# Cosine attention with a token/channel mixer on one core: no dummy products in the first slots, one transpose moved to TensorE, SyncE's transposes ahead of its loads

## The chip, the cores and the metric

The kernel runs on one core of a Trainium2 chip. The metric is the device time of one execution in microseconds; less is better. A core has TensorE (PE, matrix products and transposes, with weight loads on a second track, PEld), VectorE (DVE), ScalarE (ACT), GpSimd (POOL) and SyncE (SP, here a queue that only issues transfers). ScalarE and GpSimd issue a few transfers too. Each engine works through its own instructions in order and waits on semaphores for the others.

## The reference, cut to what matters

```python
# q, k, v: (8, 12, 448, 64) float32;  tau = 0.1
q_n = q / (norm(q, axis=-1) + 1e-6);  k_n = k / (norm(k, axis=-1) + 1e-6)
attn = softmax(q_n @ k_n.T / tau)             # per batch and head, 448 x 448
x = (attn @ v), heads side by side            # (8, 448, 768)
u = x + (relu(x.T @ w_tok1) @ w_tok2).T       # mix over the 448 tokens, 256 hidden
out = u + relu(u @ w_ch1) @ w_ch2             # mix over the 768 channels, 1536 hidden
```

## The kernel before, in words

**Tiling.** The 12 heads of a batch are taken two at a time: a pair fills 128 channels. There are 6 pairs in a batch (`NPAIR`) and 48 in all (`NP_ALL`). The pairs 0 to 11 ("old") hold a head's 448 rows as 4 groups of 112 rows; from pair 12 on, K and V are held as 3 groups of 128 rows plus a rest of 64 (`KC` = 3, the tiles `kr` and `vr`, loaded once for three pairs).

**Stages of a pair.** `load_qk` and `load_v` bring q, k and v (SP's queue; k of pairs 0 to 2 on ACT's). `square` (L240 on POOL, L238 on ACT) squares q and k, `sums` (L263, DVE) adds the squares up, `norms` (L276 to L280 on ACT, L273 and L274 on DVE) makes 1/(norm + eps), `scale` (L292 to L300, POOL) multiplies q and k by it into `kq`, in float16. `tpose` transposes `kq` on TensorE (L316) and DVE copies the result out of PSUM into `qk` (L318); from pair 13 on (`DMA_T0`) `tpose_dma` does this with one transposing transfer on SP (L324). `score` makes the products of k and q (L339, and L346 for the rest of k), ACT takes the exponential into `pt` (L340, L347). `cast_v` (L216 to L220, POOL) makes v float16. `pv_wide`, or `pv_rest` and `pv`, multiply by v (L361, L378, L396); DVE divides by the sum (reciprocal L381 or L399, product L382 or L400) and gives `x`. `tok1` (L409, relu on DVE L412) and `tok2` (L423, added to x on DVE, L426) give `u`.

**The channel mix** needs u transposed, `ut`: `udma` does this with a transposing transfer on SP (L432), `upose` with four TensorE transposes and a DVE copy (L438, L439). `m_ch1` multiplies `ut` of a whole batch, all six pairs, by w_ch1 (L448, relu on ACT L451); `m_ch2` multiplies by w_ch2 (L464), adds u on DVE (L468) and stores (L483, L489).

**Order of work.** All instructions of an engine stand in the order in which the program calls these functions. The program is a loop over slots, one for each pair i, written out by hand:

- The slots 1 to 5 (L582 to L614) hold attention alone, since no batch is complete. On TensorE a slot is: two score groups, `tok1(i-2)`, `pv_wide(i-1)`, two score groups, `tpose(i+1)`, `tok2(i-2)`, and `warm(8)` (L608): eight 128-wide products of the identity matrix with itself, which nothing reads. On SP a slot ends with `load_v(i+4)` and `udma(i-2)` (L614).
- Slot 6 is written out at L616 to L635. Slot 7 starts with three score groups, `tok2(5)`, `upose(4)` and `upose(5)`, `sums(9)`, `pv(6, ...)`, and then the first unit of the channel mix of batch 0 (L666 to L684).
- From slot 7 on, a queue of units (12 `m_ch1` and 6 or 8 `m_ch2` for a batch) is fed into the slots by a budget of estimated TensorE time (`fed`, `due`, `refill`). So TensorE always has channel work of the batch before between the steps of attention.
- `side(i)` (L639 to L664) holds the work of the other engines in slot i: loads of pair i+6 or i+7, squares, `cast_v(i)`, norms, `scaled(i+2)`, `tpose_dma(i+2)` from slot 11 on, `load_v(i+4)`. On SP the order in a slot is therefore: loads of q and k, transpose of `kq` (which waits for POOL's `scaled`), load of v, then stores and the `udma` of that slot. On POOL it is: squares, cast, scaling. `SQ_AT` says which pairs are squared where the shift from i+3 to i+5 is made: slot 12 squares the pairs 15 and 16, slot 14 the pairs 18 and 19.

**Buffers.** q and k have 7 each, v has 4, `kq` has 4, `ut` 2. In PSUM the tag "b" has 2 buffers (transposes, tok1, tok2, pv, the dummy products, some channel units) and the tag "s" has 3 (scores and wide units).

**Weights** come through POOL's queue: w_ch1 in four parts (L193), w_ch2 in two (L197), cast on the way.

Of the kernel before, what the change touches and what calls it, by code (L numbers as in the profile page):

```python
# [8 lines left out]
FP16 = mybir.dt.float16  # L9
# [13 lines left out]
def kernel(  # L23
# [12 lines left out]
    nc = tc.nc  # L36
# [11 lines left out]
    NPAIR = H // 2  # L48
    NP_ALL = B * NPAIR
# [4 lines left out]
    DMA_T0 = 13  # L54
# [34 lines left out]
    ps = ctx.enter_context(tc.tile_pool(name="ps", bufs=2, space=bass.MemoryType.PSUM))  # L89
# [4 lines left out]
    ut = {}  # L94
    u16 = {}
    gts = {}

    def old(i):
        return i < OLD
# [22 lines left out]
    def load_qk(i):  # L122
        b, h0 = i // NPAIR, 2 * (i % NPAIR)
        n = i // HP
        half.setdefault(n, {})
        st = pipe[i] = {}
        st["q"] = qkv.tile([SC, QS, E], FP32, name=f"qf_{i}", tag="qf")
        nc.sync.dma_start(out=st["q"][:].rearrange("p (g c) e -> p g (c e)", g=2),
                          in_=q[b, h0:h0 + 2].rearrange("g (p c) e -> p g (c e)", c=NCH))
        st["k"] = load_rows(i, "k", k[b], 7)  # L130
        if not old(i) and "kr" not in half[n]:
            half[n]["kr"] = load_rest(i, "k", k[b])

    def load_v(i):
        pipe[i]["v"] = load_rows(i, "v", v[i // NPAIR], 4)
        if not old(i) and "vr" not in half[i // HP]:
            half[i // HP]["vr"] = load_rest(i, "v", v[i // NPAIR])

    id16 = cst.tile([128, 128], FP16, name="id16")
# [102 lines left out]
    def squares(i):  # L242
        square(i, 0)
        square(i, 1)
# [75 lines left out]
    def tpose_dma(i):  # L320
        st = pipe[i]
        qk = att.tile([128, 2 * NCH * 128], FP16, name=f"qk_{i}", tag="qk")
        st["qk"] = qk[:].rearrange("p (a c s) -> p a c s", a=2, c=NCH)
        nc.sync.dma_start_transpose(out=st["qk"].rearrange("p a c s -> p (a c) s"),  # L324
                                    in_=st["kq16"][:].rearrange("p a c g e -> p (a c g e)"))

    def warm(n, wide=False):
        w = (ps2 if wide else ps).tile([128, 128], FP32, name=f"warm{len(pipe)}_{n}", tag="s" if wide else "b")
        for _ in range(n):
            nc.tensor.matmul(w[:], id16[:], id16[:], start=True, stop=True)  # L330
# [100 lines left out]
        b, pj = i // NPAIR, i % NPAIR  # L431
        nc.sync.dma_start_transpose(out=ut[b][:, pj], in_=u16[b][:, pj].rearrange("p m d -> p (m d)"))  # L432

    def upose(i):
        b, pj = i // NPAIR, i % NPAIR
        psT = ps.tile([128, 4, 128], FP16, name=f"psT_{i}", tag="b")
        for m in range(4):
            nc.tensor.transpose(psT[:, m], u16[b][:, pj, m], id16[:])  # L438
        nc.vector.tensor_copy(out=ut[b][:, pj], in_=psT[:])  # L439

    def m_ch1(b, ct, wide):
        if b // 2 not in gts:
# [80 lines left out]
    SQ_AT = {12: [15, 16], 13: [17], 14: [18, 19], 15: [20]}  # L523
    SU_AT = {15: [18, 19]}

    with tc.manual_schedule():
        for i in range(3):
            load_qk(i)
        load_v(0)
        load_qk(3)  # L530
        load_v(1)
        load_qk(4)
        load_v(2)
        load_qk(5)
        load_v(3)
        nc.scalar.add_instruction(mybir.InstLoadActFuncSet(
            name=nc.get_next_instruction_name(), act_func_set_id=ACT_SET_LN_EXP,
            ins=[], outs=[]))
        weights_tok1()

        square(0, 1, act=True)
        square(0, 0, act=True)
        sums(0, 1, 2)
        norms(0, 1, 1, 2)
        sums(0, 0, 1)
        norms(0, 1, 1, 2, dve=True)
        norms(0, 1, 0, 1)
        scale(0, 1, nc.vector)
        norms(0, 1, 0, 1, dve=True)
        scale(0, 0)  # L550
        square(1, 1, act=True)
        square(1, 0, act=True)
        square(2, 1, act=True)
        warm(40, True)
        sums(1)
        norms(1, 2)
        tpose(0, 1, 2)
        warm(3, True)
        tpose(0, 0, 1)
        warm(5, True)  # L560
        square(2, 0)
        weights_tok2()
        score(0, 0)
        score(0, 1)
        norms(1, 2, dve=True)
        scale(1, 0)
        scale(1, 1, nc.vector)
        sums(2)
        norms(2, 3)
        cast_v(0)  # L570
        score(0, 2)
        warm(8)
        tpose(1)
        score(0, 3)
        warm(6)
        norms(2, 3, dve=True)
        square(3, 1, act=True)
        square(3, 0)
        load_v(4)
        load_qk(6)  # L580

        for i in range(1, NPAIR):  # L582
            if i == 1:
                scale(2, 0)
                scale(2, 1, nc.vector)
            else:
                scaled(i + 1)
                if i != 3:
                    weights_ch1(max(i - 3, 0))
            load_qk(i + 6)  # L590
            score(i, 0)
            score(i, 1)
            sums(i + 2)
            norms(i + 2, i + 3)
            if i >= 2:
                tok1(i - 2)
            pv_wide(i - 1)
            norms(i + 2, i + 3, dve=True)
            cast_v(i)
            square(i + 3, 0)  # L600
            if i == 1:
                warm(10)
            score(i, 2)
            score(i, 3)
            tpose(i + 1)
            if i >= 2:
                tok2(i - 2, pe=True)
            warm(8)  # L608
            square(i + 3, 1, act=True)
            if i == 1:  # L610
                place_w2()
            load_v(i + 4)
            if i >= 2:
                udma(i - 2)  # L614

        i = NPAIR  # L616
        load_qk(i + 6)
        scaled(i + 1)
        score(i, 0)
        score(i, 1)  # L620
        sums(i + 2)
        norms(i + 2, i + 3)
        tok1(i - 2)
        pv_wide(i - 1)
        norms(i + 2, i + 3, dve=True)
        cast_v(i)
        load_v(i + 4)
        squares(i + 3)
        scaled(i + 2)
        weights_ch1(3)  # L630
        score(i, 2)
        score(i, 3)
        tpose(i + 1)
        tok1(i - 1)
        tok2(i - 2, pe=True)  # L635

        def side(i):  # L639
            single = i + 2 < SINGLE  # L640
            t = i + (6 if i <= 14 else 7)
            if t < NP_ALL:
                load_qk(t)
            for t in SQ_AT.get(i, [i + 3 if single else i + 5]):
                if t < NP_ALL:
                    squares(t)
            cast_v(i)
            if i in (8, 10):
                weights_ch2((i - 8) // 2)
            if single:  # L650
                norms(i + 2, i + 3)
                norms(i + 2, i + 3, dve=True)
            elif i + 4 < NP_ALL:
                sums(i + 4)
                if (i + 4) % HP == 2:
                    norms(i + 2, i + 5, act=True)
            if i + 2 < NP_ALL:
                scaled(i + 2)
                if i + 2 >= DMA_T0:
                    tpose_dma(i + 2)  # L660
            if i + 4 < NP_ALL:
                load_v(i + 4)
            if i == 14:
                load_qk(i + 7)  # L664

        for i in range(NPAIR + 1, NP_ALL):  # L666
            b, pj = i // NPAIR, i % NPAIR
            for c in range(KC):
                score(i, c)
            if i == NPAIR + 1:  # L670
                tok2(i - 2, pe=True)
                upose(i - 3)
                upose(i - 2)
                sums(i + 2)
            pv_rest(i - 1)
            pv(i - 1, 0)
            pv(i - 1, 1)
            if i == NPAIR + 1:
                refill(0)
            elif pj == 2 and b > 1:  # L680
                refill(b - 1)
            side(i)
            fed[0] += fed[1]
            unit(True)  # L684
            if old(i):
                score(i, KC)
            else:
                score_rest(i)
            if i > NPAIR + 1:
                tok2(i - 2)  # L690
            if i + 1 < DMA_T0:
                tpose(i + 1)
            if due():
                unit(True)
            while due():
                unit()
            tok1(i - 1)
            if i + 2 < SINGLE:
                for t in SU_AT.get(i, [i + 3]):
                    sums(t)  # L700
        last = NP_ALL - 1
        unit()
        pv_rest(last)
        pv(last, 0)
        pv(last, 1)
        unit(True)
        tok2(last - 1)
        unit(True)
        tok1(last)
        unit(True)  # L710
        unit(True)
        tok2(last)
        refill(B - 1)
        while queue:
            unit()
# [35 lines left out]
```

## Time and profile before

| what | value |
|---|---|
| median of 7 runs | 399.38 us (393.63 to 403.48) |
| the profiled execution, own time | 393.67 us |
| its span, first to last instruction | 391.9 us |
| busy in the span: TensorE, weight loads, DVE, ACT, POOL | 375.0, 244.5, 209.1, 224.9, 237.1 us |
| moved by transfers | 65.13 MB, mean 166 GB/s |
| transposing transfers: `ut<-u`, `qk<-kq` | 46, 35 |
| dummy products (`warm`) | 112, of which 40 in the slots 1 to 5 |

1.8 us of the profiled execution's time lie outside its span. That execution is among the quickest: the seven runs reach from 0.04 us below it to 9.8 us above it.

How to read what follows: times in a timeline are microseconds from the start of the span; a row gives start, duration, engine, line, operation, output<-input, shape, how many instructions were merged, and in square brackets how long the engine stood idle before them and what ended that. In the page's rows of groups, busy time and the mean duration of one instruction (ns) stand after the first bar, the idle time ahead of the group and its main cause after the second. Matmuls are pipelined, so a mean duration is longer than the time from one start to the next.

### The profile page before, as it was taken

Reading aid. Unit: us, or ns where it says so; the run is one execution under the profiler, and the core shown is the slowest. Engines: PE = TensorE matmul, PEld = TensorE weight load, DVE = VectorE, ACT = ScalarE, POOL = GpSimd, SP = SyncE. Lnnn points to the kernel's source line nnn. Section 1 sums busy time; section 2 is a strip of 40 time slices with the busy share of each in tenths; the row PEclk is TensorE's granted clock in tenths of the full one; section 3 lists DMA queues with packets and bytes.
Section 4 is the critical chain, followed back from the end, with each engine's and each line's share of the span. In section 5 each row is a group of like instructions: output and inputs, shape, how many; then the busy total and the mean of one; then the engine's idle time right before and its main releaser. Section 6 shows DMA issues by size and latency. Waiting matters only on the chain.

```text
span 391.9 us, 10212 instructions
## 1 busy us (share of the span) xinstructions
PE 375.0 (96%) x4136; PEld 244.5 (62%) x4136; DVE 209.1 (53%) x457; ACT 224.9 (57%) x378; POOL 237.1 (60%) x384
## 2 busy tenths in 40 slices
PE   6989799998999999999999999999999999999995
PEld 5667566665656666666666666667666666565563
DVE  7788766676544575465544574465544553232032
ACT  5899678845574547764674547764674546601400
POOL 8899887897788492949677492949575440000000
PEclk9999999999999999999999999999999999999999
DMA  8999999988699989875899688786796382013023
GB/s 223 263 227 227 226 268 181 224 182 190 159 222 172 198 202 217 144 185 159 182 205 175 155 211 213 149 161 139 196 213 133 66 185 69 15 48 101 0 67 96
DMA packets 117599, 65.13 MB, mean 166 GB/s; under 512 B 75440, under 2 KB 113968, under 8 KB 117552
## 3 DMA queue, kind: packets, MB, share of 16 engines
q1 hardware_dynamic: 112656, 58.54, 68.5%
q0 software_dynamic: 4080, 5.21, 7.7%
q10 hardware_dynamic: 816, 0.73, 0.7%
q8 instruction: 32, 0.52, 0.6%
q14 instruction: 15, 0.12, 0.1%
HBM read 43.45 MB, written 11.01 MB: 139 GB/s over the span
## 4 chain that ended last, share of the span: by engine, by line
PE 81%; DMA 6%; DVE 6%; ACT 3%; issue 1%; POOL 1%; SPq 1%; ACTq 0%; DVEq 0%; POOLq 0%
PE psG L448 27%; PE psF L464 25%; PE psO L378 9%; PE psS L339 7%; PE psR L409 5%; PE psU L423 4%; DMA ut<-u 3%; DMA qf<-in_q_dram 2%; PE psQ L346 2%; ACT pt L340 2%; DVE ssq L263 1%; PE psO L361 1%; DMA kf<-in_k_dram 1%; DVE ost L468 1%; PE psO L396 1%
## 5 line engine op out<-in xcount | busy, mean ns | idle before, releaser
L340 ACT ACTIVATE pt<-psS 128x896 f16<-128x896 f32 (+1 forms) x156 | 132.6, 916 | 54.2 <-PE psS L339 54.1
L448 PE MATMUL psG<-ut,wc1t 128*128 128x448 f16 x576 | 116.9, 352 | 2.0 <-DMA ut<-u 1.2
L464 PE MATMUL psF<-wc2t,gt 128*128 128x384 f16 (+2 forms) x684 | 116.4, 323 | 0.0
L464 PEld LDWEIGHTS <-gt 128*128 128x128 f16 x684 | 64.2, 98 | 38.1 <-issue 0.2
L451 ACT ACTIVATE gt<-psG 128x448 f16<-128x448 f32 x96 | 51.4, 544 | 60.7 <-PE psG L448 60.7
L292 POOL TENSOR_TENSOR kq<-kf,rn 128x384 f16<-128x384 f32 (+1 forms) x48 | 43.0, 895 | 67.1 <-ACT rn L280 59.1
L448 PEld LDWEIGHTS <-wc1t 128*128 128x128 f16 x576 | 53.9, 98 | 46.7 <-issue 2.6
L468 DVE TENSOR_TENSOR ost<-psF,u 128x384 f32<-128x384 f32 (+2 forms) x65 | 35.7, 549 | 63.7 <-PE psF L464 59.7
L263 DVE TENSOR_REDUCE ssq<-sq 128x15 f32<-128x960 f32 (+2 forms) x49 | 55.7, 1140 | 4.0 <-ACT sq L238 3.5
L412 DVE TENSOR_SCALAR rt<-psR 128x256 f16<-128x256 f32 x48 | 20.1, 419 | 61.5 <-PE psR L409 61.4
L292 POOL TENSOR_TENSOR kq<-qf,rn 112x512 f16<-112x512 f32 x45 | 47.0, 1045 | 3.0
L339 PE MATMUL psS<-qk 64*128 64x448 f16 x312 | 41.6, 359 | 2.4 <-DMA qk<-kq 1.0
L240 POOL TENSOR_TENSOR sq<-kf 128x384 f32<-128x384 f32 (+1 forms) x46 | 40.2, 873 | 4.0 <-DMA kf<-in_k_dram 4.0
L378 PE MATMUL psO<-vt,pt 128*128 128x65 f16 (+1 forms) x1056 | 40.4, 193 | 0.8 <-POOL vt L218 0.8
L240 POOL TENSOR_TENSOR sq<-qf 112x512 f32<-112x512 f32 x39 | 40.6, 1040 | 0.0
L378 PEld LDWEIGHTS <-pt 128*128 128x128 f16 (+1 forms) x1056 | 35.4, 97 | 4.5 <-issue 1.6
L382 DVE TENSOR_TENSOR x<-psO,rec 128x256 f16<-128x256 f32 x84 | 35.6, 424 | 2.9
L426 DVE TENSOR_TENSOR u<-psU,x 128x512 f16<-128x512 f32 x48 | 33.0, 687 | 5.1 <-PE psU L423 3.6
L381 DVE RECIPROCAL rec<-psO 128x4 f32<-128x4 f32 x84 | 14.8, 176 | 30.3 <-PE psO L378 30.3
L409 PEld LDWEIGHTS <-w1t 128*128 128x128 f16 x384 | 24.9, 98 | 8.6 <-issue 1.9
L423 PEld LDWEIGHTS <-w2t 128*128 128x128 f16 x384 | 24.8, 98 | 8.3 <-issue 1.5
L423 PE MATMUL psU<-rt,w2t 128*128 128x128 f16 x384 | 29.3, 219 | 0.5 <-DVE qk L318 0.2
(58 smaller groups left out, 281.6 us busy)
## 6 DMA issues: line engine op xcount, KB each, us to landing
qf<-in_q_dram SPq DMA_DIRECT2D x48, 224.0 KB, 3.9
kf<-in_k_dram SPq DMA_DIRECT2D x36, 192.0 KB, 3.2
vf<-in_v_dram SPq DMA_DIRECT2D x36, 192.0 KB, 2.9
vf<-in_v_dram SPq DMA_DIRECT2D x12, 224.0 KB, 7.6
out_dram<-ost SPq DMA_DIRECT2D x8, 336.0 KB, 3.3
wc1t<-in_moe_w_ch_dram POOLq DMA_DIRECT2D x4, 576.0 KB, 9.3
wc2t<-in_moe_w_ch_dram POOLq DMA_DIRECT2D x2, 1152.0 KB, 12.4
out_dram<-ost SPq DMA_DIRECT2D x8, 288.0 KB, 3.2
```

The lines of the kernel that those rows point to most:

```text
L240: nc.gpsimd.tensor_mul(out=dst, in0=src, in1=src)
L263: nc.vector.tensor_reduce(out=h["ssq"][0:n, col, sl], in_=pipe[i]["sq"][0:n, sl], axis=AXX.X, op=ALU.add)
L292: eng.tensor_tensor(out=kq[0:p, a, 0:n].rearrange("p c g e -> p g c e"), in0=st["kq"[a]][:].rearrange("p (g c) e -> p g c e", g=2), in1=_b ...
L339: nc.tensor.matmul(psS[:, hh, 0:S], qk[hb, c * n:c * n + 128], qm[hb], start=True, stop=True)
L340: nc.scalar.activation(out=pts[i % 2][0:n, 2 * S * c:2 * S * (c + 1)].rearrange("p (h s) -> p h s", h=2), in_=psS[0:n, :, 0:S], func=AF.Ex ...
L378: nc.tensor.matmul(psO[:, m, 0:E + 1], pts[i % 2][0:n, at:at + 128], vt[0:n, i % HP, nch * hh + c, 0:E + 1], start=(old(i) and c == 0), st ...
L409: nc.tensor.matmul(psR[:, tt], w1t[:, w1[m], tt * 128:(tt + 1) * 128], st["x"][:, m], start=(m == 0), stop=(m == 3))
L423: nc.tensor.matmul(psU[:, m], w2t[:, tt, lo:lo + 128], st["rt"][:, tt], start=(tt == 0), stop=(tt == TT - 1))
L448: nc.tensor.matmul(psG[:, 0:S], wc1t[:, dt, ct * 128:(ct + 1) * 128], ut[b][:, dt].rearrange("p m s -> p (m s)")[:, lo:lo + S], start=(dt ...
L451: nc.scalar.activation(out=gt[:, ct, (b % 2) * S:(b % 2 + 1) * S], in_=psG[:, 0:S], func=AF.Relu)
L464: nc.tensor.matmul(psF[:, 0:hi - lo], gt[:, ct, at:at + 128], wc2t[:, ct, lo:hi], start=(ct == 0), stop=(ct == CT - 1))
L468: nc.vector.tensor_tensor(out=o[p0:p1, lo:hi].rearrange("p (j e) -> p j e", e=128), in0=psF[p0:p1, 0:hi - lo].rearrange("p (j e) -> p j e" ...
```

## The change

1. `warm(8)` is taken out of the slots 1 to 5. The other dummy products (`warm` in the prologue and `warm(10)` in slot 1) stay.
2. `udma(i-2)` in those slots is issued only for i = 2, 3, 4, so pair 3 has no transposing transfer. In slot 7 `upose(3, 2)` turns the pairs 3 and 4 into one PSUM tile with eight TensorE transposes, and one DVE copy of 1024 columns takes them out. `upose(5)` follows as before.
3. In `side(i)` from slot 11 on (`i + 2 >= DMA_T0`), `load_qk` moves from the front to behind `tpose_dma(i+2)`, still ahead of `load_v(i+4)`. Where two pairs are squared in a slot (slots 12 and 14), the second is squared after `scaled(i+2)` in place of ahead of `cast_v(i)`.

```diff
-    def upose(i):
+    def upose(i, n=1):
         b, pj = i // NPAIR, i % NPAIR
-        psT = ps.tile([128, 4, 128], FP16, name=f"psT_{i}", tag="b")
-        for m in range(4):
-            nc.tensor.transpose(psT[:, m], u16[b][:, pj, m], id16[:])
-        nc.vector.tensor_copy(out=ut[b][:, pj], in_=psT[:])
+        psT = ps.tile([128, n, 4, 128], FP16, name=f"psT_{i}", tag="b")
+        for j in range(n):
+            for m in range(4):
+                nc.tensor.transpose(psT[:, j, m], u16[b][:, pj + j, m], id16[:])
+        nc.vector.tensor_copy(out=ut[b][:, pj:pj + n], in_=psT[:])
...
                 tok2(i - 2, pe=True)
-            warm(8)
             square(i + 3, 1, act=True)
...
-            if i >= 2:
+            if 2 <= i < NPAIR - 1:
                 udma(i - 2)
...
             t = i + (6 if i <= 14 else 7)
-            if t < NP_ALL:
+            if t < NP_ALL and i + 2 < DMA_T0:
                 load_qk(t)
-            for t in SQ_AT.get(i, [i + 3 if single else i + 5]):
-                if t < NP_ALL:
-                    squares(t)
+            sq = [n for n in SQ_AT.get(i, [i + 3 if single else i + 5]) if n < NP_ALL]
+            for n in sq[0:1]:
+                squares(n)
             cast_v(i)
...
                 if i + 2 >= DMA_T0:
                     tpose_dma(i + 2)
+            for n in sq[1:]:
+                squares(n)
+            if t < NP_ALL and i + 2 >= DMA_T0:
+                load_qk(t)
             if i + 4 < NP_ALL:
                 load_v(i + 4)
...
                 tok2(i - 2, pe=True)
-                upose(i - 3)
+                upose(i - 4, 2)
                 upose(i - 2)
```

## The prediction

> **What bounds the kernel now.** I read the page first, then TensorE's timeline for every gap, then the timeline of all engines around each gap, and SP's and POOL's timelines for the order of their queues.
>
> ```profile
> PE 375.0 (96%) x4136; PEld 244.5 (62%) x4136; DVE 209.1 (53%) x457; ACT 224.9 (57%) x378; POOL 237.1 (60%) x384
> DMA  8999999988699989875899688786796382013023
> L448 PE MATMUL psG<-ut,wc1t 128*128 128x448 f16 x576 | 116.9, 352 | 2.0 <-DMA ut<-u 1.2
> ```
>
> TensorE is busy 96% of the span, so the time can only come from its gaps and from dummy work. The second row shows when the transfer engines are full: nearly without a break for the first fifth of the span. From 113 us to its last product TensorE waits under 2 us in all, by its timeline. Its gaps lie in two places: the slots 1 to 7, and 87 to 112 us.
>
> ```profile
> 31.88 0.61 PE L330 MATMUL warm<-id 128*128 128x128 f16 x8 [0.45 <-DVE qk L318]
> 36.43 0.61 PE L330 MATMUL warm<-id 128*128 128x128 f16 x8 [0.45 <-DVE qk L318]
> 46.97 0.73 PE L448 MATMUL psG<-ut,wc1t 128*128 128x448 f16 x3 [1.23 <-DMA ut<-u]
> 87.33 0.74 PE L339 MATMUL psS<-qk 64*128 64x448 f16 x6 [0.26 <-DMA qk<-kq]
> 94.80 0.74 PE L339 MATMUL psS<-qk 64*128 64x448 f16 x6 [0.77 <-DMA qk<-kq]
> 96.51 0.91 PE L378 MATMUL psO<-vt,pt 128*128 128x65 f16 x24 [0.85 <-POOL vt L218]
> 107.05 0.62 PE L423 MATMUL psU<-rt,w2t 128*128 128x128 f16 x8 [0.22 <-DVE x L382]
> 111.66 1.30 PE L448 MATMUL psG<-ut,wc1t 128*128 128x448 f16 x6 [0.58 <-ACT gt L451]
> ```
>
> Each row's bracket is a wait that the change could touch. The two first rows are 4.55 us apart: that is a slot's period.
>
> **Part 1, the dummy products.** In the slots 2 to 5 they start only when DVE has copied `qk` (31.27 + 0.56 = 31.83), and the scores that need the same copy stand behind them: 31.88 to 32.42, so 0.54 us of TensorE per slot on the loop TensorE, DVE, TensorE. In slot 1 they start before that copy is made (17.57 against 18.39) and cost nothing. The most to be had is 4 x 0.54 = 2.2 us. But ACT is almost full:
>
> ```profile
> 28.29 1.73 ACT L340 ACTIVATE pt<-psS 112x896 f16<-112x896 f32 x2 [0.24 <-PE psS L339]
> 32.83 1.73 ACT L340 ACTIVATE pt<-psS 112x896 f16<-112x896 f32 x2 [0.24 <-PE psS L339]
> 37.37 1.73 ACT L340 ACTIVATE pt<-psS 112x896 f16<-112x896 f32 x2 [0.25 <-PE psS L339]
> ```
>
> ACT idles 0.24 us a slot, the rest is back to back (two pairs of exponentials 1.73 + 1.71, norms, one square 0.63). So it becomes the bound at a period of 4.30: 0.15 (slot 3) + 0.24 + 0.24 + 0.25 = 0.9 us. TensorE can run a little further ahead of ACT, some 0.2, until a score waits for its PSUM buffer. POOL is also full here (it has 0.3 us of idle in the slots 2 to 5), but its `kq` is ready 1.1 us before the transposes that read it (33.90 against 34.96). I take **-1.0**, bounds 0 and -2.2, nearer the ACT rows.
>
> Here a rule speaks against the change. The row: the first 40 dummy products take 311 ns each, start to start 105 ns; those from 15 us on take 219 and start every 55. So TensorE began at half rate, though the granted clock is shown as 1.00 from the first window on; the duration is the witness. The Trainium skill (TensorE: Matmul & The Clock Gate, "A second HAM failure mode: psum-queue depth-cycling") says that frequent micro-idling between groups can make the clock swing between half and full rate; its section "Why this matters for your kernels" names gaps above about 3 us. By the first, four slots with some 3.5 us of real products would take 7 us each, +10 us; by the second, nothing, since the gap left is 0.5 to 0.8 us. This trace has a gap of 1.23 us at 46.97 with full-rate products (352 ns) behind it, so I take 0.
>
> **Part 2, u of pair 3.** The first channel product needs all six `ut`. TensorE did three of them at 45.01, and then waited for pair 3's transfer, issued at 36.99 and landed 9.93 us later. That wait, 1.23, goes. Added: four TensorE transposes (about 0.23 us at 55 ns each), which fit in the 0.56 us that TensorE waits at 43.59 for u of pair 5; and on DVE a copy of 1024 columns (0.68, as `qk` at 74.06) for one of 512 (0.41), +0.27. The next PSUM tile, pv's, needs that buffer: TensorE starts pv at 44.2 for 43.92, so +0.28. Sum **-0.95**. What is late next is pair 2's transfer: issued at 32.45, 11.8 us to landing, 44.25. With both parts TensorE gets there at 45.01 - 1.0 + 0.28 = 44.29: it just clears. If it lands where it did, part 1 can't yield more than 1.0; bounds of both parts together -0.9 and -2.4. On SP a blocked transpose issue (36.99 to 40.05) goes too, so the loads of pair 12 start some 3 us sooner.
>
> **Does this lead of 1.95 survive?** Between 47 and 87 us everything but the transfers moves with TensorE. The tightest is the second half of w_ch2: issued at 65.52, 12.7 us to landing, 78.22; TensorE first reads it at 78.2, with no room at all.
>
> ```profile
> 65.52 0.87 POOL L197 DMA_DIRECT2D wc2t<-in_moe_w_ch_dram  x1
> 68.52 0.57 SPq L128 DMA_DIRECT2D qf<-in_q_dram  x1
> 69.14 0.45 SPq L110 DMA_DIRECT2D kf<-in_k_dram  x1
> 76.53 1.23 SPq L324 DMA_TRANSPOSE qk<-kq  x1
> ```
>
> But part 3 takes the loads of pair 17 (416 KB, rows two and three) out of this stretch: they go behind the transpose at 76.5. The skill (DMA: Bandwidth & Descriptors, "Issuing engines are not separate DMA queues") has SyncE's and GpSimd's transfers interleave on the same 16 engines, and this trace agrees (k of pair 17 needs 10.0 us while w_ch2 runs, 2.9 at 82 us). At the stretch's 195 GB/s, 416 KB are 2.1 us: w_ch2 lands near 76.1 and is wanted at 76.25. I take 0; if this cover fails, up to 1.95.
>
> **Part 3, SP's and POOL's order.** Times without the lead. Slot 12: pair 16's squares (0.83 + 0.29 + 1.04, about 2.05 in all) leave the front, POOL's `scaled(14)` ends at 82.1 for 84.2, its transpose (3.1 us) lands at 85.3, wanted at 87.07: the 0.26 goes. Slot 13: POOL's order evens out; the transpose of pair 15 goes out at 89.6, as before, but ahead of pair 19's 416 KB and at the usual 1.2 us for 2.59; it lands by 93, for 94.7: the 0.77 goes. Slot 14:
>
> ```profile
> 93.94 0.83 POOL L240 TENSOR_TENSOR sq<-kf 128x384 f32<-128x384 f32 x1 [2.37 <-DMA kf<-in_k_dram]
> 95.96 0.51 POOL L218 CAST vt<-vf 128x384 f16<-128x384 f32 x1
> ```
>
> POOL waited 2.37 us for k of pair 19 with the cast of v and `scaled(16)` behind it. With those squares last, the cast is done at 92 and the 0.85 goes. Sum -1.88. The price: loads of q and k go out later, up to `scaled`'s end. Pair 20's go out at 96.0 and 96.6 for 94.3; with 3.3 us for k they land at 99.9, POOL squares until 102.0 and casts v and its rest until 102.8, where TensorE wants the rest at 104.37 - 1.88 = 102.5: **+0.3**. The waits of 0.22 and 0.58 behind it come from DVE's two sums of 2.20 us and stay; they swallow part of that. From pair 22 on, q and k are squared two slots (14 us) after they are loaded; loads moved back by a transpose and POOL's wait (up to 5 us, 217.94 to 223.00) are hidden there. Loads of v and the `udma` keep their place behind both. Without the 14 us each late load would stall POOL. Part 3: **-1.7**, bounds +0.8 and -1.9.
>
> **Sum.** -1.0 - 0.95 - 1.7 = -3.65: span 388.25, with the 1.77 around it 390.0 against its own 393.67, 0.9%. The median of the runs is 5.7 above that execution. If that surplus is TensorE's waiting for transfers, the gain is rather larger than smaller; I subtract about the same from it: **395.6**.
>
> **Rivals.**
> - *Larger*: in runs with slower transfers the waits at 47, 78, 87 and 95 us are longer, and the 416 KB and one transpose less before 79 us are worth more. For it: the spread of 9.85 us at one clock. Against: no such run is profiled. Some -6.5: 392.9. 17%.
> - *Swallowed*: pair 2's transfer and w_ch2 land where they land, parts 1 and 2 yield about nothing or are given back at 78 us, part 3 remains with its late squares: -1.5, 397.9. For it: landings of 11.8 and 12.7 us and a full DMA row. 22%.
> - *Slower*: the clock. If it falls back in the slots 2 to 5, +10 less the other parts' 2.65 is +7.4: 406.8. It decides from two half-rate slots on (+5 against -3.65). Against it the gap at 46.97. 11%.
>
> **How the numbers follow.** The forecast case, 394.4 to 396.9, has 50%. About 1%, 4 us, is what a measurement of this kernel can tell from no change. Half the forecast case lies beyond it, 25%, and all of "larger", 17%: faster 0.42. The other half and "swallowed": same 0.47. Slower 0.11. The range runs from within "larger", 391.0, to no change with the median's own scatter, 399.8; it leaves out "slower" and the end of "larger".
>
> **What would show it.** Right: the slots 3 to 6 about 4.3 us long with ACT without gaps, 128-wide products still 219 ns; the first channel group in one piece near 44.3; no wait at w_ch2's middle; scores of the slots 14 and 15 and pv of slot 15 without gaps; a short wait on the cast of v near 100. Wrong: products of 311 ns in the slots, a wait on pair 2's `ut`, on w_ch2, or POOL's squares waiting for k past 100 us by more than 3 us.

## The result, and the profile after

| | median of all runs | range | runs |
|---|---|---|---|
| before | 398.13 us | 392.42 to 405.02 | 59 |
| after | **390.88 us** | 389.30 to 394.40 | 24 |
| profiled execution: own time, span, before | 393.67, 391.9 | | |
| profiled execution: own time, span, after | 389.30, 387.5 | | |

The ratio of after to before is **0.9885**, 95% interval 0.9864 to 0.9907. It leaves out every run that lies over 1.5% above the quickest of its kernel; here these are long runs of the kernel before, so it shows less than the medians of all runs do (0.982), and the reason why there are so many of them is the main finding below.

The page of the changed kernel, its busy times, the transfers' row and the channel products:

```profile
PE 371.8 (96%) x4100; PEld 241.5 (62%) x4100; DVE 208.9 (54%) x457; ACT 224.4 (58%) x378; POOL 237.2 (61%) x384
DMA  8999999989697779858888697877998393023023
L449 PE MATMUL psG<-ut,wc1t 128*128 128x448 f16 x576 | 116.6, 352 | 0.2 <-ACT gt L452 0.2
```

TensorE's work fell by 3.2 us and its span by 4.4. The products of the channel mix no longer wait for `ut`. (From `upose`'s inner loop, L437, on, its lines and those of the channel mix stand one further down than before.) TensorE's timeline, in the places that the prediction showed:

```profile
26.18 0.55 PE L339 MATMUL psS<-qk 64*128 64x448 f16 x4 [0.43 <-DVE qk L318]
30.36 0.55 PE L339 MATMUL psS<-qk 64*128 64x448 f16 x4 [0.43 <-DVE qk L318]
...
42.98 1.30 PE L449 MATMUL psG<-ut,wc1t 128*128 128x448 f16 x6
...
83.78 0.74 PE L339 MATMUL psS<-qk 64*128 64x448 f16 x6 [0.28 <-DMA qk<-kq]
91.18 0.74 PE L339 MATMUL psS<-qk 64*128 64x448 f16 x6 [0.71 <-DMA qk<-kq]
100.95 0.30 PE L361 MATMUL psO<-vt,pt 64*128 64x65 f16 x8 [0.94 <-POOL vt L220]
103.26 0.61 PE L423 MATMUL psU<-rt,w2t 128*128 128x128 f16 x8
110.36 1.29 PE L449 MATMUL psG<-ut,wc1t 128*128 128x448 f16 x6
```

The two first rows are a slot apart, 4.18 us (before 4.55). The first channel group comes in one piece. The two waits on transposes that were to go are there, shifted with everything else: 0.28 for 0.26, 0.71 for 0.77. The wait on the cast of v before the 128-deep products (0.85 at 96.51) is gone and a new one of 0.94 stands ahead of the rest of v; the two waits behind it (0.22 and 0.58) are gone.

Comparing the starts of the same instructions in the two traces gives the gain by place (after less before, us): first score of slot 2 -0.81 (the last scores of slot 1, ahead of any edit, already -0.80; 0.56 of it is the landing of the first q, 3.09 for 3.65); `psU` of slot 7 -2.24; end of the first channel group -3.43; behind w_ch2's middle -3.58; slot 16 -4.53; end -4.4. So, without the start: part 1 **-1.43**, part 2 **-1.19**, w_ch2 **-0.16**, part 3 **-0.95**, the end +0.13. Sum -3.6.

These places hold for one execution of each kernel. A second profiled execution of the changed kernel (own time 390.51, `after_again` below) has its waits elsewhere:

```profile
76.69 1.14 PE L465 MATMUL psF<-wc2t,gt 128*128 128x384 f16 x6 [0.67 <-DMA wc2t<-in_moe_w_ch_dram]
102.27 0.30 PE L361 MATMUL psO<-vt,pt 64*128 64x65 f16 x8 [1.16 <-POOL vt L220]
```

There TensorE waits for w_ch2's second half and for no transpose. A wait of under 1 us that comes or goes between two kernels can therefore be chance.

### The profile page after: what moved, and what is told of

Same layout as the page of the kernel before. It is cut to its first block, busy times and chain, and to the rows that moved or that the text cites. A ratio compares the mean times of both kernels' runs of the same rounds, so it can differ in the third digit from the quotient of the medians.

```text
span 387.5 us, 10129 instructions
## 1 busy us (share of the span) xinstructions
PE 371.8 (96%) x4100; PEld 241.5 (62%) x4100; DVE 208.9 (54%) x457; ACT 224.4 (58%) x378; POOL 237.2 (61%) x384
## 4 chain that ended last, share of the span: by engine, by line
PE 81%; ACT 7%; DMA 4%; DVE 3%; POOL 2%; issue 1%; SPq 1%; POOLq 0%; ACTq 0%; DVEq 0%
PE psG L449 27%; PE psF L465 26%; PE psO L378 9%; PE psS L339 7%; ACT pt L340 5%; PE psU L423 5%; PE psR L409 4%; DMA qk<-kq 2%; PE psQ L346 2%; PE psO L361 1%; ACT sq L238 1%; DVE ost L469 1%; DMA kf<-in_k_dram 1%; POOL sq L240 1%; DVE ssq L263 1%
```

## The experiments

### One part at a time, and parts 1 and 2 together

Four kernels, made from the kernel before, on one chip; its own median there was 401.79 us (393.66 to 406.54, 28 runs).

Part 1 alone:

```diff
             if i >= 2:
                 tok2(i - 2, pe=True)
-            warm(8)
             square(i + 3, 1, act=True)
```

> Part 1 alone: the eight dummy products of slots 1 to 5 are gone, all else is as before. Own theory: ACT becomes the bound, the slots 2 to 5 are 4.19 us long instead of 4.55 (its instructions overlap by 0.11 when they stand back to back, so more than the 0.24 of idle is won), TensorE is 1.4 to 1.6 us earlier at the first channel product, and pair 3's transfer moves along with its issue: -1.4 us in all (ratio 0.9965). Rival 'transfer-bound': pair 3's u lands where it landed (46.9 us), the wait of 1.23 us grows to some 2.7 and the gain is 0 (1.000). Rival 'clock': 128-wide products of 311 ns in the slots, +10 us.

Measured: 398.17 us (394.67 to 404.39, 22 runs), ratio 1.0028, 0.9987 to 1.0068: no difference. (The medians of all runs differ by 3.6 us, but that is the number of long runs: 11 of 22 lie above 398 us, 21 of 28 of the kernel before.) TensorE's timeline of its profiled execution (own time 401.24):

```profile
26.77 0.55 PE L339 MATMUL psS<-qk 64*128 64x448 f16 x4 [0.43 <-DVE qk L318]
30.96 0.55 PE L339 MATMUL psS<-qk 64*128 64x448 f16 x4 [0.43 <-DVE qk L318]
...
43.37 0.73 PE L448 MATMUL psG<-ut,wc1t 128*128 128x448 f16 x3
52.46 1.28 PE L448 MATMUL psG<-ut,wc1t 128*128 128x448 f16 x3 [8.36 <-DMA ut<-u]
```

The slots are 4.19 long, as in the full change, and then TensorE waits 8.36 us for pair 3's transfer, issued at 35.7 and landed 16.7 us later. Removing the dummies shortens the slots as it should, but in this execution a later transfer ends last and nothing is gained.

Part 2 alone (`upose(3, 2)` and no `udma(3)`, lines of the change's second part only):

> Part 2 alone: u of pair 3 turned on TensorE, dummies and SP's order as before. Own theory: the wait of 1.23 us on u of pair 3 goes, pv of slot 7 waits 0.2 to 0.3 on the wider copy: -1.2 us (0.997). Rival 'transfer-bound': pair 2's transfer or the second half of w_ch2 (both as late as before) take it back: between 0 and -0.3.

Measured: **393.72 us** (393.44 to 395.72, 6 runs), ratio 0.9875, 0.9827 to 0.9924. In the median of all runs this one part is worth 8 us, in the profile of before only 1.23. The long runs are gone.

Parts 1 and 2 together (both edits):

> Parts 1 and 2 without part 3: pair 17's q and k are loaded before w_ch2 has landed, as before. Own theory: -2.6 us up to 70 us, but w_ch2's second half is then late, since only part 3 takes 416 KB out of its way: a wait of 1 to 2 us inside the first group of the second channel product, and -1.0 to -1.6 in all (0.996 to 0.9975). If transfers do not matter there, no such wait and -2.6 (0.9935).

Measured: 392.69 us (390.94 to 393.64, 6 runs), ratio 0.9833, 0.9782 to 0.9885. By these medians, of six runs each, part 1 is now worth 1.0. In the profiled execution pair 2's transfer ended last:

```profile
44.29 0.54 PE L449 MATMUL psG<-ut,wc1t 128*128 128x448 f16 x2
45.55 0.92 PE L449 MATMUL psG<-ut,wc1t 128*128 128x448 f16 x4 [0.72 <-DMA ut<-u]
```

Part 3 alone (the edits in `side` only):

> Part 3 alone: SP's and POOL's order from pair 13 on; dummies and pair 3's transfer as before. Own theory after seeing the changed kernel's trace: -0.95 us there (pv's wait of 0.85 and the two waits of 0.22 and 0.58 go, 0.94 of waiting for the cast of v comes, the waits of 0.26 and 0.77 on transposes stay because SP's queue is behind), plus 0.16 at w_ch2: -1.1 (0.997). By the prediction: -1.7 (0.9957). Further: if the 416 KB taken from w_ch2's way are what makes the changed kernel's runs agree better than those of before, this kernel's runs spread over some 5 us and not 10, and its median gains more than its profile.

Measured: 399.19 us (393.02 to 403.98, 6 runs), ratio 0.9888, 0.9801 to 0.9975. What part 3 is worth can't be read here: the profiled execution (own time 400.78) has the long wait too. Its TensorE timeline shows what such a wait costs besides:

```profile
44.99 0.73 PE L448 MATMUL psG<-ut,wc1t 128*128 128x448 f16 x3
53.58 1.27 PE L448 MATMUL psG<-ut,wc1t 128*128 128x448 f16 x3 [7.85 <-DMA ut<-u]
...
55.99 2.44 PE L448 MATMUL psG<-ut,wc1t 128*128 128x448 f16 x6
...
62.90 2.44 PE L448 MATMUL psG<-ut,wc1t 128*128 128x448 f16 x12
```

Six products took 2.44 us at 56 us, as long as twelve at 63: TensorE runs at half rate behind the wait. By stretch, for the same kernel (columns: stretch, its length, busy time of PE, PEld, DVE, ACT, POOL, granted clock, transfer share, GB/s):

```profile
45.00:50.00 5.00, 0.72 (x8) 0.28 (x5) 1.92 (x7) 0.52 (x2) 3.96 (x5) 0.81 1.30 127
50.00:55.00 5.00, 1.43 (x5) 0.36 (x4) 0.00 (x0) 0.11 (x1) 2.59 (x4) 0.50 1.15 190
55.00:60.00 5.00, 5.00 (x46) 2.86 (x45) 1.70 (x3) 2.62 (x4) 0.00 (x0) 0.67 1.15 232
60.00:100.00 40.00, 40.00 (x506) 26.41 (x503) 27.81 (x69) 29.42 (x52) 32.03 (x52) 1.00 0.90 184
```

The granted clock, 0.50 during the wait, is back at full only near 58 us: some 4.7 us of products take twice their time, so a wait of 7.85 costs about 10 (7.85 and half of 4.7, an estimate).

What follows: over all runs of this study, those of kernels with pair 3's transfer (the kernel before, part 1 alone, part 3 alone and the variant of the next section) lie above 398 us in 119 of 203 cases; of 104 runs of the kernels without it, none does (highest 395.72). The surplus of the median over the profiled execution comes from this one transfer and from what its lateness sets off.

### Why is pair 3's transfer late?

The kernel before, with the loads of slot 5 behind the transfer in place of ahead of it:

```diff
-            load_qk(i + 6)
+            if i < NPAIR - 1:
+                load_qk(i + 6)
...
-            load_v(i + 4)
+            if i < NPAIR - 1:
+                load_v(i + 4)
             if i >= 2:
                 udma(i - 2)
+            if i == NPAIR - 1:
+                load_qk(i + 6)
+                load_v(i + 4)
```

> The kernel before, with the loads of slot 5 (q and k of pair 11, v of pair 9, 640 KB) issued behind pair 3's transposing transfer in place of ahead of it. The instructions are the same. Theory A (pair 3's transfer is late because of the bytes queued ahead of it on SyncE's queue): 640 KB at the 145 to 190 GB/s of that stretch are 3.4 to 4.4 us, so it lands that much sooner, the wait at the first channel product shrinks from up to 8 us to about 4 or less, and the median falls from some 400 to 396 or 397. Rival B (it is late because of the transfers that share the 16 engines, w_ch1 on GpSimd's queue and pair 2's own transpose, whatever stands ahead of it in its queue): the transfer still lands 14 us or more behind its issue in most runs, and the median stays at about 400.

Measured: 395.06 us (392.26 to 403.10, 22 runs) against 401.35 of the kernel before on the same chip (55 runs). The ratio without the long runs shows no difference (0.9995, 0.9959 to 1.0031): what changed is their number, 7 of 22 above 398 us for 42 of 55. The loads that now stand behind are three of 224 KB, so 672 KB and not 640. In its profile, of a quick execution (394.85), the transfer landed 8.0 us behind its issue, where the quick execution of the kernel before has 9.9, and TensorE didn't wait; no long execution of this kernel was profiled. Theory A holds for the greater part: what stands ahead in SyncE's queue decides how often the transfer is very late. It is not the only cause, since seven runs are long still. Part of the lead then runs into waits further on (1.21 at w_ch2's middle, 1.08 and 1.06 on transposes, in that profile).

What the transfer itself does to the others is seen in the transfers' row in slices of 0.375 us, here from 37 to 52 us, for part 3 alone (pair 2's transfer landed at 42.5, pair 3's at 53.6):

```profile
DMA  9950096999997999999999989999900009996999
GB/s 284 137 40 23 12 42 36 46 46 42 42 42 38 152 238 242 205 261 249 236 220 259 229 184 216 328 273 163 18 14 14 16 13 31 41 76 68 109 148 191
```

Ahead of each landing is a stretch, here of 4.1 and 3.4 us, in which all the engines together move 12 to 76 GB/s, against 184 to 328 between the two. In the quick profiled execution of the kernel before there is one such stretch for both landings, 1.5 us long (42.25 to 43.75, 7 to 90 GB/s). The changed kernel has one between 32 and 51 us, pair 2's: 36.5 to 39.75, at most 116 GB/s but for one slice, landed 40.7.

### Part 1 taken out of the full change

The changed kernel with `warm(8)` back in its place:

> The changed kernel with the eight dummy products of the slots 2 to 5 put back; nothing else differs. Theory A (the dummies are worth what the traces of before and after show once pair 3's transfer is off the path: 0.36 us a slot): slots 4.54 long again instead of 4.19, the first channel product 1.4 us later, the whole 1.4 us slower than the changed kernel, some 392.3. Rival B (the slots' time is slack, as in the kernel that only removed the dummies: the transfers of pair 2 and w_ch2 set the pace): the same time as the changed kernel, 390.9, within 0.5. Either way no wait above 1 us on ut.

Measured: 391.45 us (390.85 to 392.75, 16 runs), ratio to before 0.991, 0.9879 to 0.9942. The slots are 4.54 long again (22.93, 27.47, 32.02), 1.4 us in all, but the median is only 0.6 above that of the changed kernel (0.75 above its repeat below): between the two theories. By the medians, about half of what the slots give reaches the end.

### The two halves of part 3

The changed kernel, with q and k loaded ahead of the transposes again, squares still last:

```diff
-            if t < NP_ALL and i + 2 < DMA_T0:
+            if t < NP_ALL:
                 load_qk(t)
...
-            if t < NP_ALL and i + 2 >= DMA_T0:
-                load_qk(t)
```

> The changed kernel, with only one of the third part's two moves: the second squares of a slot stay last, but loads of q and k go out ahead of the transposes again, as before the change. Theory A (what the transposes wait for is mainly POOL, whose squares stood ahead of the scaling; the order on SyncE's queue matters little, as the loads ahead take 1.1 us to issue): the 0.28 and 0.71 on transposes grow by at most 0.5 each, while k of pair 20 goes out earlier and the 0.94 on the cast of v goes: within 0.5 us of the changed kernel. Rival B (the order on SyncE's queue is what helps: 416 KB ahead of each transpose at 200 GB/s are 2 us): the waits on the transposes of pairs 14, 15 and 16 grow by 1 to 2 us each, and the second half of w_ch2 is late again; 2 to 4 us slower than the changed kernel.

Measured: 392.33 us (390.88 to 394.71, 6 runs) against 390.70 for the changed kernel repeated in the same group:

> The changed kernel itself, unchanged, as the yardstick on the chip of the other runs of this group. Both theories: 390.9 within 0.6 us, and all runs within some 5 us of each other; a median of 392 or more would mean that the kernels of the earlier groups (391.45 with the dummies back, 392.13 with v on ScalarE) can't be held against 390.88.

(390.25 to 392.11, 6 runs, as close to 390.88 as expected.) The profiled execution of the kernel with the loads ahead is the longest of its six, and one wait stands out in it:

```profile
88.44 1.30 PE L339 MATMUL psS<-qk 64*128 64x448 f16 x6 [2.75 <-DMA qk<-kq]
```

It is the first score of slot 14, 2.75 where the changed kernel has 0.28 in one profiled execution and none in the other, and the waits of 0.22 and 0.58 are back. The row also shows six products in 1.30 us, where the changed kernel needs 0.74. The stretches of the same kernel (columns as above):

```profile
84.00:88.00 4.00, 1.69 (x21) 1.23 (x19) 2.93 (x6) 0.83 (x3) 3.74 (x8) 1.00 0.56 111
88.00:90.00 2.00, 1.56 (x17) 0.80 (x18) 0.00 (x0) 0.96 (x2) 2.00 (x4) 0.61 0.88 213
90.00:92.00 2.00, 2.00 (x27) 1.60 (x27) 1.14 (x4) 1.97 (x4) 0.36 (x1) 0.54 0.91 244
92.00:96.00 4.00, 4.00 (x32) 2.60 (x30) 1.73 (x5) 0.56 (x2) 3.17 (x5) 1.00 1.09 224
```

The wait of 2.75 halves the clock for some 3.5 us behind it. The medians differ by 1.6 us, nearer to theory B than to A, but the six runs of each overlap (three of them lie under 391.5), one transpose was late and not three, and w_ch2 was not late. That SyncE's order matters is likely; how much is not shown.

### What is left of the waits: SyncE's queue or the engines behind it?

In the first profiled execution of the changed kernel SyncE issues back to back around those waits. Its queue's timeline:

```profile
79.92 1.25 SPq L324 DMA_TRANSPOSE qk<-kq  x1
...
84.78 1.23 SPq L432 DMA_TRANSPOSE ut<-u  x1
86.11 0.98 SPq L484 DMA_DIRECT2D out_dram<-ost  x2
87.19 1.34 SPq L324 DMA_TRANSPOSE qk<-kq  x1
```

POOL had finished `kq` at 78.87 and 86.24; both transposes went out 1 us later. The changed kernel, with v and its rest of the pairs 15 to 18 issued by ScalarE:

```diff
-        pipe[i]["v"] = load_rows(i, "v", v[i // NPAIR], 4)
+        eng = nc.scalar if 15 <= i <= 18 else None
+        pipe[i]["v"] = load_rows(i, "v", v[i // NPAIR], 4, eng)
```

(and the same for the rest of v.)

> The changed kernel, with the loads of v (and its rest) of the pairs 15 to 18 issued by ScalarE in place of SyncE. Theory A (the two waits on transposes that the change left, 0.28 at 83.8 and 0.71 at 91.2 us, come from SyncE's queue, which issues back to back from 73 to 100 us and sends the transposes 1 us after POOL's kq is ready): taking five issues out of it sends each transpose about 1 us sooner; the 0.28 and most of the 0.71 go, some 0.8 us faster. Rival B (the transposes land late because the 16 engines are full, not because they are issued late): they are issued sooner but land when they did, the waits stay, no gain; ACT's issues may even delay an exponential by 0.1 to 0.5 us each.

Measured: 392.13 us (391.14 to 394.46, 22 runs), ratio to before 0.9933, 0.9904 to 0.9963: not faster, rather slower. Both waits on transposes are gone, as A said, but so they are in the repeat of the changed kernel, where SyncE still issues those loads and sent the two transposes 0.03 and 0.41 us after `kq` was ready. The run therefore doesn't show their cause. A longer wait stands at the cast of v:

```profile
76.91 1.14 PE L466 MATMUL psF<-wc2t,gt 128*128 128x384 f16 x6 [0.39 <-DMA wc2t<-in_moe_w_ch_dram]
103.23 0.30 PE L362 MATMUL psO<-vt,pt 64*128 64x65 f16 x8 [1.77 <-POOL vt L221]
```

k of pair 20 landed 5.3 us behind its issue (3.6 in the changed kernel); POOL waited 4.69 us for it with the cast queued behind. The two loads of v before it had landed by 94.4, before k went out at 94.97; the 96 KB of their rest landed by 97.3. What the trace shows is a stretch of at most 12 GB/s from 95.2 to 96.6, ahead of the landing of slot 14's transpose at 97.9; in the changed kernel such a stretch (4 to 29 GB/s) was over at 94.7, 0.35 us after k's issue. Why the transpose was later here is open.

### Two versions on top of the change

Pair 20's loads ahead of slot 14's transpose, the sums of pair 18 a slot earlier:

```diff
-    SU_AT = {15: [18, 19]}
+    SU_AT = {14: [17, 18], 15: [19]}
...
-            if t < NP_ALL and i + 2 < DMA_T0:
+            if t < NP_ALL and (i + 2 < DMA_T0 or i == 14):
                 load_qk(t)
...
-            if t < NP_ALL and i + 2 >= DMA_T0:
+            if t < NP_ALL and i + 2 >= DMA_T0 and i != 14:
                 load_qk(t)
```

> The changed kernel, with the loads of pair 20 ahead of slot 14's transpose as they were before the change, and the sums of pair 18 in slot 14 instead of 15. Theory A (the 0.94 us that pv waits for the cast of v in slot 15 comes from POOL's squares waiting for k of pair 20, which goes out behind transpose and sums): that wait goes, the 0.22 and 0.58 that it swallowed don't come back since one of DVE's two sums runs a slot earlier; some 0.7 to 0.9 us faster than the changed kernel, 390.0. Rival B (those loads ahead make slot 14's transpose later, as in the kernel before): the wait of 0.71 at slot 15's first score grows to 1.2 or more, no gain.

Measured: 389.65 us (388.77 to 389.89, 6 runs), ratio to before 0.9868, 0.9809 to 0.9927. Of the 0.94 a wait of 0.47 is left (the repeat of the changed kernel has 1.16 there), the 0.22 and 0.58 have not come back, and 0.49 stands at w_ch2's middle. Near A. That no wait on a transpose is left says little, since the repeat has none either.

That version, with pair 2's u turned on TensorE as well:

```diff
-            if 2 <= i < NPAIR - 1:
+            if i == NPAIR - 1:
+                upose(i - 3)
+            elif i >= 2 and i < NPAIR - 2:
                 udma(i - 2)
```

> The kernel with pair 20's loads early (389.65), and u of pair 2 turned on TensorE as well, at the end of slot 5 (four transposes and a copy of 512 columns on DVE), so that no transposing transfer of u goes out between 31 and 50 us. Theory A (a transposing transfer keeps all 16 engines at 8 to 60 GB/s for 1.5 to 4 us, so each one less lets everything queued behind it land that much sooner): w_ch2's second half lands 1.5 us or more sooner, its wait of 0.49 goes, and no run is late by pair 2's transfer: 389.2, spread under 2 us. Rival B (the transfers hold it up nowhere any more, or DVE's extra copy of 0.41 us lengthens the slot): the same within 0.4, or up to 0.4 slower.

Measured: **388.80 us** (388.57 to 390.56, 6 runs), ratio to before 0.9803, 0.9751 to 0.9856, the lowest median of all. It is 1.9 below that of the changed kernel on the same chip, for both edits together; the 0.85 below the version with the first edit alone is a comparison across chips, and the ranges overlap. TensorE's timeline has no wait from 44 us to one of 0.29 at 137.82. The transfers' row from 41 to 51 us, in slices of 0.25 us:

```profile
GB/s 244 238 271 361 375 362 341 263 231 240 250 188 295 273 281 205 241 281 197 217 207 215 209 238 224 190 246 215 246 197 330 328 357 356 301 208 254 267 253 225
```

No slice is under 188 GB/s, nor is one from 32.5 to 41, and w_ch2's halves land in 9.7 and 11.1 us (12.9 and 13.2 with the first edit alone). This is as theory A has it: with the transposing transfers of u go the stretches of low rate in this part, and what was queued behind them lands sooner.

### No dummies anywhere

The changed kernel without the other 72 dummy products too (`warm` calls of the prologue and slot 1 taken out):

> The changed kernel without any of the dummy products, the 72 ahead of the first scores and in slot 1 included. Theory A (TensorE reaches its full clock after some microseconds of work and keeps it through the gaps of 0.4 us; dummies in the prologue only bring that moment forward): products of the first slot run at half rate (128 columns in 311 ns in place of 219) some microseconds longer, but ACT and DVE set the pace there; 0 to 1.5 us slower than the changed kernel. Rival B (the clock needs dense products to be granted and, once lost, is not regained in slots that leave TensorE idle 0.4 us at a time and wait): half rate through the slots 1 to 6, 7 to 10 us slower.

Measured: 391.74 us (389.60 to 393.38, 6 runs) against 390.70. As theory A says. Four scores of slot 1 still run at half rate at 14.23 us (0.93); in the changed kernel they take 0.55 at 13.24 in one profiled execution, and 0.93 at 14.54 in the other.

TensorE's timeline without dummies:

```profile
14.23 0.93 PE L339 MATMUL psS<-qk 64*128 64x448 f16 x4 [0.23 <-DVE qk L318]
...
18.80 0.55 PE L339 MATMUL psS<-qk 64*128 64x448 f16 x4 [0.73 <-DVE qk L318]
```

Full rate is there from the scores at 16.85 us on (four in 0.72) and stays through the slots; in the two executions of the changed kernel the granted clock is back at full near 12.7 and 15.6 us. Its profile has 1.36 us of waiting for pair 2's transfer, so the 1.0 us isn't the clock alone; the ranges overlap.

## Why the prediction was right, and where it was off

**The sum** against the profiled execution was -3.65, with 390.0 for own time; measured 389.30, of which 0.8 is an earlier start. That the sum of the places, -3.6, fits so well is luck: the parts 1 and 2 gave 0.67 more than said, part 3 gave 0.75 less. **The median** was to fall by "about the same", to 395.6; it fell from 398.13 to 390.88, by 7.25, just under the low end of the stated range, 391.0. (As a ratio, 0.9905 was forecast; the ratio without the long runs is 0.9885, that of the medians 0.982.) That is the step that failed: the text says that the surplus of 5.7 makes the gain "rather larger than smaller" if it is TensorE's waiting for transfers, and then sizes this at nothing. It was mainly that. The rival *Larger* (17%, 392.9) had the mechanism, and named the wait at 47 us first among its four; in both long executions that were profiled it was mainly this one, with 7.9 and 8.4 us and half-rate products behind it. The working could have seen it: a spread of 9.85 us is most likely a wait that the quick execution hardly has, and the largest wait on a transfer in the profile is the first candidate. "At one clock" did not hold either: of the 28 runs of the kernel before beside part 1, those above 400 us had a mean granted clock of 0.975 to 0.991, those under 398 one of 0.990 to 0.999, as half rate behind a long wait would make it.

**Part 1.** Predicted -1.0, -1.43 in the trace. That ACT becomes the bound was right; its period was mis-sized. In the changed kernel:

```profile
26.33 0.63 ACT L238 ACTIVATE sq<-qf 112x512 f32<-112x512 f32 x1
26.85 1.73 ACT L340 ACTIVATE pt<-psS 112x896 f16<-112x896 f32 x2
28.44 0.33 ACT L276 ACTIVATE rn<-ssq,tiny 112x16 f32<-112x16 f32 x1
```

An instruction that finds its input ready starts 0.11 to 0.14 us before the one ahead ends (26.85 against 26.33 + 0.63 = 26.96). With an idle gap of 0.24 closed, that overlap is gained as well: 0.36 a slot. And alone the part is worth nothing that can be measured (0.13% faster to 0.68% slower): the bound of 0 was the right one for the kernel before, whose pair 3 transfer is later than the slots.

**The clock.** The value 0 was right. Without the dummies TensorE waits 0.43 us a slot and its products stay at full rate. From slot 2 on, waits of 0.94, 1.36 and 1.77 us had full-rate products behind them, those of 2.75, 7.85 and 8.36 half-rate ones. "Why this matters for your kernels" (the Trainium skill, TensorE: Matmul & The Clock Gate), which puts the limit at about 3 us, agrees in kind; the one wait of 2.75 was enough here. The length of one wait is not all, as the prologue of the changed kernel shows:

```profile
7.13 0.37 PE L316 MATMUL pst<-id,kq 112*128 112x112 f16 x4 [1.12 <-DVE kq L292]
...
9.43 1.30 PE L339 MATMUL psS<-qk 64*128 64x448 f16 x6 [0.20 <-DVE qk L318]
```

The four transposes run at full rate, then the six scores at half (1.30 for 0.74, granted clock 0.50 from 9.4 to 12.4), though between the first dummy product and them no wait is longer than 1.12 us. So a swing of the kind that the section on "psum-queue depth-cycling" describes was seen, in the prologue of nine of the fourteen profiled executions and in none of their slots 2 to 5. The rival *Slower* had the effect in the wrong place: it came behind the wait on pair 3's transfer, in both long executions that were profiled, and once behind a late transpose.

**Part 2.** Predicted -0.95, -1.19 in the trace: 1.39 less at the first channel group, 0.20 for the wider copy (predicted 0.28). That pair 2's landing at 44.25 caps both parts was wrong in this profile: issued 1.52 sooner, it took 9.8 for 11.8 us and landed at 40.73. In parts 1 and 2 together it did cap them, by 0.72.

**w_ch2.** Predicted 0, with the 416 KB of pair 17 as cover. No wait in the profile after; 0.67 in the repeat's, 0.39 and 0.49 in two variants. Cover there is, but it is used up in some executions. That may be one reason why only about half of part 1's 1.4 reached the end; no run separates it.

**Part 3.** Predicted -1.7, measured -0.95 by trace; 1.8 to 2.3 by medians (392.69 to 390.88, and 393.72 to 391.45), so the size of the term is open. The 0.85 of pv went as said. The 0.26 and 0.77 were to go and stayed in the first profiled execution, while the repeat has neither. In the first the working moved the transposes ahead of the loads of their own slot, but not past what was left in SyncE's queue of the slot before (the `udma` and the stores ahead of 87.19). The lead of 3.5 us had also moved the wanted times forward, which the working, in times "without the lead", left out. The price was late k of pair 20, as named, 0.94 (1.16 in the repeat) for 0.3; for it the 0.22 and 0.58, which were to stay, were swallowed whole: DVE's two sums of 2.20 us ran at 99.71, while TensorE waited. POOL waited 3.52 us for that k, longer than the 3 us that the prediction named as a sign of being wrong, though until 98.08 and not past 100.

```profile
98.08 0.83 POOL L240 TENSOR_TENSOR sq<-kf 128x384 f32<-128x384 f32 x1 [3.52 <-DMA kf<-in_k_dram]
...
100.55 0.35 POOL L220 CAST vt<-vr 128x192 f16<-128x192 f32 x1
```

**Open.** Why the stretch of low rate lasts 1.5 us in one execution and 4 in another, and why a third of the runs stays long with 672 KB less ahead of the transfer, no run here shows.

## What to carry to other kernels

When the runs of a kernel spread by more than the waits in its profile, the profile may be of a quick one: ask of each wait on a transfer whether it could make the spread, do not cost it by its size in that execution alone, and ask whether the change takes it away. Here a transfer with nothing between its landing and its use was worth replacing by work on an engine although the trace showed only a small wait, and a part that gained on an engine ahead of that transfer was worth nothing until this was done. Profile the same kernel twice before a wait of under 1 us is put down to an edit: two executions of the changed kernel had such waits in different places.

## What the runs showed of the hardware that was not expected

- In the slots 2 to 7 a transposing transfer of u (128 KB) has a stretch of low rate for all transfers ahead of its landing: 4.1 and 3.4 us at 12 to 76 GB/s in part 3 alone, 1.5 us at 7 to 90 in the kernel before. That the transfer makes it is concluded from its absence where the transfer is absent. By stretches of 5 us from 31 to 51, the rate was 225 to 268 GB/s in the kernel that turns the pairs 2 and 3 on TensorE, and 98 to 193 in part 3 alone.
- The time to issue a transfer varies with the execution: pair 3's transpose took SyncE 3.06 us in the kernel before, 2.29 in part 3 alone and 1.19 in the kernel that has 672 KB less ahead of it. Two loads of 48 KB (`kr`) behind it took 6.57 and 6.02 us in the two long executions, and 3.64 in the kernel before.
- The clock falls to half behind a wait of 2.75 us (for 3.5 us) as behind one of 7.85 (for 4.7 us); behind a single one of 1.77 it doesn't. In the prologue it fell with no wait longer than 1.12 us.
- Instructions that stand back to back on ScalarE overlap by 0.11 to 0.14 us.
